# Low key rows of each quad copied by a small DMA of SyncE's queue, and another order of the words ahead of chunk 2

## The chip, the cores and the metric

The kernel runs on one core of a Trainium2 chip. The core has five engines, each with its own queue of instructions worked off in order: TensorE (PE; the loading of its weights is shown apart as PEld), VectorE (DVE), ScalarE (ACT), GpSimd (POOL) and SyncE (SP), which only issues DMAs here; GpSimd issues DMAs too. The metric is the device time of one execution in microseconds, as the median of several runs.

## What is computed

The reference is an attention with a forget gate, followed by an MLP. Cut to what matters:

```python
q, k, v: (8, 8, 576, 64); f: (8, 8, 576); w_in: (512, 2048); w_out: (2048, 512)
cum   = cumsum(log(clip(f, 1e-4, 1)), axis=-1)
s     = q @ k.T / sqrt(64) + cum[..., :, None] - cum[..., None, :]
s     = where(above the diagonal, -1e9, s)
attn  = softmax(s) @ v
x     = attn as (8 * 576, 8 * 64)
h     = x @ w_in
out   = gelu_tanh(h) @ w_out              # (4608, 512)
```

The kernel takes the decay out of the softmax: exp(cum[q] - cum[k]) is a factor of the query, which cancels in the division, and a factor of the key, `wT = exp(-cum)` (with a constant shift), which is multiplied into the values (`vw`) and into the column that gives the denominator (`w_bf`).

## The kernel before

**Tiles.** The 64 heads are worked in 16 quads of four heads (quads 2b and 2b+1 are batch b). The 4608 rows of the MLP are worked in nine chunks of 512. A quad's queries and keys are loaded (L208), transposed by VectorE (L214), and multiplied by TensorE into scores in PSUM (L277) in rounds of up to 512 columns per head; ScalarE takes their exp into `pt` (L285); the triangles on the diagonal are cut either by GpSimd (L291) or by a product on VectorE (L321); then TensorE multiplies `pt` with `w_bf` (denominators) and with `vw` (values) at L333 (quads 0 and 1, in halves) or L347 (all others). VectorE transposes and inverts the denominators (L366 to L370) and writes the attention's output into `xT` (L379). The score tiles share a PSUM pool of two slots: a whole round takes both, half a round one.

**Low key rows.** Quads from 2 on pack the first 64 keys and the last 64 keys into blocks of their own. The block "low" has its keys in partitions 64 to 127, so the first 64 rows of the weighted values are wanted a second time, in those partitions: `copy_low` (L236) copies `vw[i % 2][0:64, 0]` to `vw[i % 2][64:128, LOW]`, once per quad, 14 times in all (quads 2 to 15). It reads what `make_vw` (L231) has written, and the value products of that quad (L347) read it.

**MLP.** The first product is L395 (L419 for chunk 0, in halves and quarters; L468 and L520 where seven products of sums stand for eight), its gelu is ScalarE's. The second product is L667 for chunk 0 and L600 for the others. The latter two are generators: they are pulled a few matmuls at a time, as filler between the attention's steps. Results go to HBM by SyncE (L625, L673).

**Loads.** q, k, both weights and batch 0 and 1 of v are issued by GpSimd, the rest of v by SyncE.

**The order by hand.** The whole program is a list of words, run once from left to right; each engine's queue gets its instructions in that order. After the setup come SETUP and FRONT (all up to chunk 1), then for the chunks 2 to 7 SECOND, STEADY (three times), FLUSH and LAST. The first number of a word is a quad, a chunk or a part:

| word | what | engine that it queues on |
|---|---|---|
| TQ.i, TK.i | transpose the queries, the keys of quad i | VectorE |
| S.i.r, H.i.r.g | round r of the scores of quad i, whole or heads 2g and 2g+1, with its exp | TensorE, ScalarE |
| M, m | cut triangles: M.i.r.keys, m.i.r.keys | GpSimd, VectorE |
| D.i, V.i.x, v.i.x | denominators; value product x (even or odd columns), with a third number the half of quads 0 and 1 | TensorE, then VectorE |
| VW.i, vw.i | weighted values | GpSimd, VectorE |
| CL.i | `copy_low` | VectorE |
| CW | cumulative sums of log f (L719, L721) and their exp | TensorE, ScalarE |
| W | cast `wT` to `w_bf` | VectorE |
| TR, tr | cast the triangles for m | VectorE, ScalarE |
| Z | zeros in padding rows | GpSimd |
| J.h.g, j | quarter g of the first product of chunk 0 for its half h, with its gelu (j leaves the gelu to GJ) | TensorE, ScalarE |
| I.c.p | eighth p of the first product of chunk c, with its gelu | TensorE, ScalarE |
| F.c.n, f.c.n | n pulls of the second product of chunk c; F with weights of 128 columns, f with four of 32 | TensorE, then VectorE and SyncE |
| G, U, UW, PW, T | sums for the seven products, on VectorE (PW on GpSimd) | VectorE, GpSimd |
| LK.i, LQ.i, LP, LC, WI, WO | loads of keys, queries, v of batch 0, v of batch 1, w_in, w_out | GpSimd |
| LV, LB | loads of v | SyncE |
| B.n.cols | n filler matmuls of so many columns, whose result is not used (L256) | TensorE |
| X, Y | load ScalarE's table of exp, of gelu | ScalarE |

A word with @ waits for the end of another one. The code that runs a word:

```python
for word in table.split():
    word, _, gate = word.partition("@")
    name, *args = word.split(".")
    ...
    did = ops[name](*args)
    ...
    if gate:
        after(did[0], dmas[gate])
```

Of the kernel before, what the change touches and what calls it, by code (L numbers as in the profile page):

```python
# [16 lines left out]
def kernel(  # L17
# [10 lines left out]
    nc = tc.nc  # L28

    B, H, S, D = q.shape  # L30
# [36 lines left out]
    LOW, HIGH = NT, NT - 1  # L67
# [5 lines left out]
    """  # L73

    FRONT = """
        Z TQ.0 LP.2 TR WI.1 TQ.1 S.0.0 B.1.384 CW WI.0 TK.1 S.0.2 LP.4 LP.3 B.1.512 vw.0.0 B.2.512 H.1.0.1 H.1.1.1 WI.3 M.0.0 W vw.1.0 WI.2 B.2.512
        WI.5 LQ.2 WI.4 H.1.0.0 D.0.0 M.1.0.1 M.1.0.0 H.0.1.1 V.0.0.0 H.0.1.0 M.0.1 WI.6 V.0.1.0 B.2.256 H.1.1.0 B.1.256 D.1.0 H.0.3.0 B.1.256 V.1.0.0 H.0.3.1
        WI.7 LK.2 V.1.1.0 m.0.3.2 H.1.3.0 j.0.0 vw.0.1 H.1.3.1 LC.1.4 WO.0 m.0.3.4 WO.1 D.0.1 M.1.3 S.1.2 M.1.1 VW.1.1 V.0.0.1 V.0.1.1 LC.1.2 D.1.1
        J.0.1 J.0.2 WO.2 LC.1.0@VW.1.1 WO.3@m.0.3.2 V.1.0.1 V.1.1.1 LC.1.1 GJ.0.0 LC.1.3 TK.2 J.1.1 LK.3 J.0.3 J.1.0 LQ.3 TQ.2 LQ.4 VW.3
        J.1.3 LK.4 J.1.2 F.0.4 X F.0.4 S.2.0 F.0.11 TK.3 S.2.2 F.0.6 LV.2.0 TQ.3 F.0.4 LK.5 S.2.1 F.0.2 F.0.7 TQ.4 m.2.1 S.3.0 vw.2 CL.2 M.2.2 f.0.7  # L80
        M.2.0 D.2 S.3.1 f.0.7 LQ.5 V.2.0 m.3.0 S.3.2 TK.4 LK.6@LQ.4 f.0.1 f.0.3 V.2.1 M.3.2 f.0.2 S.4.1 CL.3 m.3.1 LQ.6 f.0.5 TQ.5 H.4.2.1 D.3 H.4.0.1
        H.4.0.0 VW.4 V.3.1 v.3.0 f.0.1 H.4.2.0 U.0 m.4.1 LV.2.1@m.3.1 I.1.1 LQ.7@CL.3 I.1.4 TQ.6 I.1.6 m.4.2.3 I.1.0 m.4.2.2 I.1.5 CL.4 U.3 LV.3.0@LQ.7
        U.1 TK.6 I.1.2 M.4.0 U.2 G.0 TK.5 UW.2.1 I.1.3 I.1.7 G.1.1.2 F.1.16 X UW.2.2 S.5.0 UW.2.3 LQ.8 F.1.19 S.5.1 D.4 VW.5 M.5.0 f.1.13 S.5.2 V.4.0
        f.1.14 V.4.1 UW.2.4 m.5.2.3 m.5.2.2 CL.5 M.5.1 S.6.0 f.1.13 D.5 S.6.1 f.1.4 LK.7 V.5.1 f.1.3 f.1.10 vw.6 S.6.2 m.6.1 M.6.2.2 m.6.0 V.5.0
        LV.3.1@LK.6 f.1.5 CL.6 LK.8 m.6.2.3
    """

    SECOND = """
# [32 lines left out]
    def many(n, shape, dtype, name):  # L121
        return [singles.tile(shape, dtype, name=f"{name}{i}") for i in range(n)]
# [11 lines left out]
    vw = many(2, [128, NT + 1, 4, D], BF16, "vw")  # L134
# [98 lines left out]
            wT[:, i, t0:t1, :].unsqueeze(3).to_broadcast([128, t1 - t0, 4, D]))  # L233

    def copy_low(i):
        return nc.vector.tensor_copy(vw[i % 2][64:128, LOW], vw[i % 2][0:64, 0])  # L236

    def key_columns(i, key, h, c):

# [511 lines left out]
    def load_values(b, half):  # L751
# [16 lines left out]
        "VW": lambda i, *part: make_vw(i, nc.gpsimd, *part),  # L768
        "vw": lambda i, *part: make_vw(i, nc.vector, *part),
        "CL": copy_low,  # L770
        "TK": transpose_k,
        "TQ": transpose_q,
# [86 lines left out]
```

## Time and profile before

| | |
|---|---|
| median of three runs | 323.59 us (323.31 to 323.96) |
| the profiled execution | 323.22 us |
| its span, first to last instruction | 321.4 us |
| granted TensorE clock | 1.000 |
| TensorE busy | 309.6 us |
| VectorE busy | 242.0 us |
| ScalarE busy | 212.7 us |
| GpSimd busy | 107.8 us |
| L236, the copy of the low key rows | 14 times, 0.22 us each |

Times are microseconds from the start of the span. A row of a timeline has the start, the time until the last of the merged instructions ended, the engine, the line, the operation, output and inputs, and the number of instructions; in brackets stands the idle time of the engine before it and what ended it. Matmuls overlap, so the time that a group costs TensorE is read from its start to the start of the next group. In lists of groups a row ends with the busy time in us and the mean of one in ns. In lists of DMA issues the last number is the median time from issue to landing, in us.

Where the words lie in time: quads 0 and 1 take TensorE from 8.6 to 31.9 us, the rest of the first product of chunk 0 until 40.7, quads 2 and 3 with the second product of chunk 0 until 66.2, the first product of chunk 1 until 80.1, quads 4 and 5 and part of 6 with the second product of chunk 1 until 100.7. With the first product of chunk 2 the list SECOND begins.

### The profile page before, as it was taken

What the parts mean: (1) busy time and instruction counts of PE and PEld (TensorE: products, weight loads), DVE (VectorE), ACT (ScalarE), POOL (GpSimd) and SP (SyncE); (2) the same over time, 40 slices, a digit from 0 to 9 for tenths busy, and PEclk for the clock granted to TensorE, in tenths of its full rate; (3) what the DMA queues carried; (4) which work ended last, traced back from release to release, by engine and by line L of the source; (5) the groups of instructions that cost most, each with busy time, mean ns of one, the idle gap of its engine ahead of it and who ended that gap; (6) DMA issues with size and microseconds to landing.
All of it is one profiled execution on the core that took longest, in us unless ns stands there. A gap on an engine that the chain in (4) does not pass through costs nothing.

```text
span 321.4 us, 11820 instructions
## 1 busy us (share of the span) xinstructions
PE 309.6 (96%) x5339; PEld 220.7 (69%) x5339; DVE 242.0 (75%) x374; ACT 212.7 (66%) x242; POOL 107.8 (34%) x145
## 2 busy tenths in 40 slices
PE   0899999999999999999999999999999999999996
PEld 0557844544776567776788878767776786688785
DVE  4765337898979879779877987699876866597674
ACT  4676576775766776878767866787586744836610
POOL 8989343522301416400851075205610140000000
PEclk9999999999999999999999999999999999999999
DMA  7999999585126931593139411971011111010203
GB/s 126 218 210 208 247 213 199 104 155 109 35 43 129 227 78 37 116 209 72 39 82 228 87 39 35 190 172 36 7 47 53 37 34 37 30 37 0 100 33 99
DMA packets 47490, 33.41 MB, mean 104 GB/s; under 512 B 29776, under 2 KB 42192, under 8 KB 47440
## 3 DMA queue, kind: packets, MB, share of 16 engines
q0 software_dynamic: 9632, 15.99, 28.3%
q1 hardware_dynamic: 37664, 16.60, 19.1%
q8 instruction: 41, 0.67, 0.9%
q14 instruction: 9, 0.07, 0.1%
q10 hardware_dynamic: 144, 0.07, 0.1%
HBM read 36.85 MB, written 9.44 MB: 144 GB/s over the span
## 4 chain that ended last, share of the span: by engine, by line
PE 91%; ACT 3%; DVE 3%; DMA 2%; issue 1%; POOL 0%; DVEq 0%; POOLq 0%
PE ps_w L600 30%; PE ps_h L395 19%; PE ps_s L277 9%; PE po L347 9%; PE ps_q L520 8%; PE pso L667 4%; PE ps_h L419 4%; PE ps_u L468 4%; DMA q_c<-in_q_dram 2%; PE po_m L333 1%; ACT pt L285 1%; ACT gT L403 1%; DVE xT L379 1%; PE idle_ps L256 1%; PE cum_ps L721 1%
## 5 line engine op out<-in xcount | busy, mean ns | idle before, releaser
L285 ACT ACTIVATE pt<-ps_s 128x1024 bf16<-128x1024 f32 (+2 forms) x100 | 94.0, 990 | 38.6 <-PE ps_s L277 35.9
L291 POOL TENSOR_SCALAR_AFFINE_SELECT pt<-pt 128x512 bf16<-128x512 bf16 (+3 forms) x65 | 41.4, 647 | 95.2 <-ACT pt L285 72.3
L395 PE MATMUL ps_h<-xT,w_in_sb 128*128 128x512 bf16 (+1 forms) x320 | 66.8, 358 | 0.3 <-ACT gT L403 0.2
L395 PEld LDWEIGHTS <-w_in_sb 128*128 128x128 bf16 x320 | 31.2, 98 | 26.6 <-issue 0.6
L600 PEld LDWEIGHTS <-gT 128*32 128x32 bf16 (+1 forms) x1216 | 44.1, 97 | 5.5 <-issue 2.2
L403 ACT ACTIVATE gT<-ps_h 128x1024 bf16<-128x1024 f32 x34 | 34.6, 1017 | 18.7 <-PE ps_h L395 18.4
L600 PE MATMUL ps_w<-w_out_sb,gT 128*32 128x256 bf16 (+1 forms) x1008 | 42.6, 273 | 0.0
L277 PE MATMUL ps_s<-qT,kT 32*128 32x64 bf16 (+5 forms) x896 | 36.3, 263 | 3.2 <-DVE qT L214 3.0
L600 PEld LDWEIGHTS <-gsum 128*32 128x32 bf16 (+1 forms) x948 | 35.4, 97 | 3.8 <-issue 1.5
L231 POOL TENSOR_TENSOR vw<-v_nat,wT 128x1280 bf16<-128x1280 f32 (+1 forms) x13 | 29.6, 2279 | 11.7 <-DMA v_nat<-in_v_dram 11.4
L536 DVE TENSOR_TENSOR usnap<-ps_q,usnap 128x1024 f32<-128x1024 f32 x15 | 17.9, 1222 | 18.6 <-PE ps_q L520 13.2
L277 PEld LDWEIGHTS <-kT 32*128 32x128 bf16 x896 | 16.5, 93 | 19.6 <-issue 10.1
L600 PE MATMUL ps_w<-usum,gsum 128*32 128x256 bf16 (+1 forms) x791 | 30.0, 273 | 0.0
L617 DVE COPY snap<-ps_w 128x512 f32<-128x512 f32 x32 | 21.8, 681 | 6.2 <-PE ps_w L600 6.0
L531 ACT ACTIVATE gT<-usnap 128x1024 bf16<-128x1024 f32 x15 | 15.8, 1054 | 12.1 <-DVE usnap L536 11.8
L379 DVE TENSOR_TENSOR xT<-po,rb 128x576 bf16<-128x576 f32 x26 | 19.5, 752 | 5.6 <-PE po L347 5.3
L347 PE MATMUL po<-pt,vw 128*32 128x64 bf16 (+4 forms) x624 | 22.4, 278 | 0.0
L214 DVE STREAM_TRANSPOSE qT<-q_c 128x576 f32<-128x576 f32 x16 | 19.8, 1246 | 1.7 <-DMA q_c<-in_q_dram 1.7
L347 PEld LDWEIGHTS <-vw 128*32 128x32 bf16 x672 | 14.6, 97 | 9.4 <-issue 2.8
L214 DVE STREAM_TRANSPOSE kT<-k_c 128x576 f32<-128x576 f32 x16 | 19.5, 1246 | 1.9 <-DMA k_c<-in_k_dram 1.9
L208 POOL DMA_DIRECT2D k_c<-in_k_dram x16 | 9.1, 568 | 33.6 <-DVE kT L214 18.0
L520 PEld LDWEIGHTS <-w_in_sb 128*128 128x128 bf16 x160 | 15.6, 98 | 2.5 <-issue 0.4
(135 smaller groups left out, 478.5 us busy)
## 6 DMA issues: line engine op xcount, KB each, us to landing
out_dram<-o_st SPq DMA_DIRECT2D x35, 256.0 KB, 2.3
k_c<-in_k_dram POOLq DMA_DIRECT2D x16, 288.0 KB, 5.3
q_c<-in_q_dram POOLq DMA_DIRECT2D x16, 288.0 KB, 6.3
v_nat<-in_v_dram SPq DMA_DIRECT2D x16, 256.0 KB, 5.4
v_nat<-in_v_dram SPq DMA_DIRECT2D x20, 128.0 KB, 5.1
v_nat<-in_v_dram POOLq DMA_DIRECT2D x8, 256.0 KB, 8.1
w_in_sb<-in_moe_w_in_dram POOLq DMA_DIRECT2D x8, 256.0 KB, 7.8
w_out_sb<-in_moe_w_out_dram POOLq DMA_DIRECT2D x4, 512.0 KB, 11.3
```

Source lines behind the costliest of these rows:

```text
L214: return nc.vector.transpose(out=dst.rearrange("p s c -> p (s c)").bitcast(FP32) .rearrange("p (t a) -> p a t", a=S // 32), in_=src.rearra ...
L231: return eng.tensor_mul(vw[i % 2][:, t0:t1], vb[:, t0:t1, h0:h0 + 4, :], wT[:, i, t0:t1, :].unsqueeze(3).to_broadcast([128, t1 - t0, 4, D]))
L277: nc.tensor.matmul(tiles[h // 2][:, h % 2, c0:c0 + nq], key_columns(i, key, h, c), qq[32 * h:32 * h + 32, q0:q0 + nq, c], start=(c == 0 an ...
L285: nc.scalar.activation(p[:, 2 * g:2 * g + 2, off:off + n], t[:, :, 0:n], AF.Exp, scale=scale)
L291: nc.gpsimd.affine_select(out=x, in_=x, compare_op=ALU.is_ge, fill=0.0, base=0, pattern=pattern, channel_multiplier=-1)
L347: nc.tensor.matmul(po[r0:r0 + w.shape[-1], 448 + q0:448 + q0 + nq], w, p[:, h, col:col + nq], start=(key in (0, "low")), stop=(key in ("lo ...
L379: nc.vector.tensor_mul(xT[:, 2 * u + x, r0 + s0:r0 + s1], po, rbs[i, part])
L395: nc.tensor.matmul(ph[:, j, n * cols:(n + 1) * cols], w_in_sb[:, dt, 128 * ft:128 * ft + 128], xT[:, dt, h0:h0 + cols], start=(dt == 0 and ...
L403: nc.scalar.activation(gelus(c, 2 * pr, 2), ph, AF.Gelu_apprx_tanh)
L520: nc.tensor.matmul(ps[:, k, HC * n:HC * n + HC], w[:, d, 128 * n:128 * n + 128], x[:, d, :], start=(first and n == 0 and d == 0), stop=(d ...
L600: nc.tensor.matmul(ps[c0:c0 + width, n, cols[0]:cols[1]], x[:, j, 128 * n + c0:128 * n + c0 + width], w[:, j, cols[0]:cols[1]], start=(fir ...
L617: copy(kept[name], ps)
```

## The change

`copy_low` issues a DMA in SyncE's queue, where it was a copy on VectorE. This holds for all 14 quads. The list FRONT is replaced by another one; SETUP, SECOND, STEADY, FLUSH and LAST stay. The new FRONT has the same loads, scores, products and sums, with these differences in kind: the triangles are cast by ScalarE (tr for TR); M.0.0, M.0.1, M.2.2 and M.5.0 become m; m.2.1, m.3.1, m.4.2.2, m.4.2.3, m.5.2.3, m.6.0, m.6.1 and m.6.2.3 become M; UW.2.1 becomes PW.2.1; there are 21 filler words B with 6,912 columns in all for 7 with 3,968; pulls of the second products are split into smaller pieces.

```diff
     FRONT = """
-        Z TQ.0 LP.2 TR WI.1 TQ.1 S.0.0 B.1.384 CW WI.0 TK.1 S.0.2 LP.4 LP.3 B.1.512 vw.0.0 B.2.512 H.1.0.1 H.1.1.1 WI.3 M.0.0 W vw.1.0 WI.2 B.2.512
-        WI.5 LQ.2 WI.4 H.1.0.0 D.0.0 M.1.0.1 M.1.0.0 H.0.1.1 V.0.0.0 H.0.1.0 M.0.1 WI.6 V.0.1.0 B.2.256 H.1.1.0 B.1.256 D.1.0 H.0.3.0 B.1.256 V.1.0.0 H.0.3.1
-        WI.7 LK.2 V.1.1.0 m.0.3.2 H.1.3.0 j.0.0 vw.0.1 H.1.3.1 LC.1.4 WO.0 m.0.3.4 WO.1 D.0.1 M.1.3 S.1.2 M.1.1 VW.1.1 V.0.0.1 V.0.1.1 LC.1.2 D.1.1
-        J.0.1 J.0.2 WO.2 LC.1.0@VW.1.1 WO.3@m.0.3.2 V.1.0.1 V.1.1.1 LC.1.1 GJ.0.0 LC.1.3 TK.2 J.1.1 LK.3 J.0.3 J.1.0 LQ.3 TQ.2 LQ.4 VW.3
-        J.1.3 LK.4 J.1.2 F.0.4 X F.0.4 S.2.0 F.0.11 TK.3 S.2.2 F.0.6 LV.2.0 TQ.3 F.0.4 LK.5 S.2.1 F.0.2 F.0.7 TQ.4 m.2.1 S.3.0 vw.2 CL.2 M.2.2 f.0.7
-        M.2.0 D.2 S.3.1 f.0.7 LQ.5 V.2.0 m.3.0 S.3.2 TK.4 LK.6@LQ.4 f.0.1 f.0.3 V.2.1 M.3.2 f.0.2 S.4.1 CL.3 m.3.1 LQ.6 f.0.5 TQ.5 H.4.2.1 D.3 H.4.0.1
-        H.4.0.0 VW.4 V.3.1 v.3.0 f.0.1 H.4.2.0 U.0 m.4.1 LV.2.1@m.3.1 I.1.1 LQ.7@CL.3 I.1.4 TQ.6 I.1.6 m.4.2.3 I.1.0 m.4.2.2 I.1.5 CL.4 U.3 LV.3.0@LQ.7
-        U.1 TK.6 I.1.2 M.4.0 U.2 G.0 TK.5 UW.2.1 I.1.3 I.1.7 G.1.1.2 F.1.16 X UW.2.2 S.5.0 UW.2.3 LQ.8 F.1.19 S.5.1 D.4 VW.5 M.5.0 f.1.13 S.5.2 V.4.0
-        f.1.14 V.4.1 UW.2.4 m.5.2.3 m.5.2.2 CL.5 M.5.1 S.6.0 f.1.13 D.5 S.6.1 f.1.4 LK.7 V.5.1 f.1.3 f.1.10 vw.6 S.6.2 m.6.1 M.6.2.2 m.6.0 V.5.0
-        LV.3.1@LK.6 f.1.5 CL.6 LK.8 m.6.2.3
+        LC.1.4 B.1.256 WI.4 B.1.256 TQ.0 B.1.256 TK.1 B.1.128 tr CW B.1.512 B.1.256 S.0.2 B.1.512 B.1.128 TQ.1 LP.2 LP.3 H.1.0.1 WI.1 S.0.0 B.1.256 B.1.256 B.1.256 B.1.128 B.1.512 B.1.256 B.1.128 H.1.1.1 B.2.512 vw.0.0 vw.1.0 m.0.0 B.2.512 WI.0 W H.1.0.0 H.0.1.0 D.0.0 B.1.128 B.1.128 V.0.0.0 LQ.2 LP.4 H.0.1.1 WI.5 B.1.256 V.0.1.0 Z WI.2 M.1.0.0 H.1.1.0 M.1.0.1 B.1.256 D.1.0 H.0.3.0 V.1.0.0 H.0.3.1 m.0.1 V.1.1.0 WI.6 WI.7 WO.0 H.1.3.0 WI.3 M.1.1 j.0.0 H.1.3.1 m.0.3.2 LK.2 m.0.3.4 vw.0.1 D.0.1 WO.3 V.0.0.1 M.1.3 WO.1 S.1.2 V.0.1.1 VW.1.1 J.0.2 D.1.1 WO.2 GJ.0.0 J.0.3 V.1.0.1 V.1.1.1 J.0.1 J.1.3 J.1.0 TQ.2 TK.2 U.0 J.1.2 LC.1.1 LK.3 LC.1.0@VW.1.1 F.0.3 LC.1.2 F.0.1 X LC.1.3 F.0.1 S.2.0 f.0.1 LQ.3 LK.4 f.0.1 F.0.1 TK.3 F.0.5 LQ.4 F.0.3 S.2.2 F.0.4 U.1 F.0.1 TQ.3 F.0.1 J.1.1 VW.3 LQ.5 vw.2 LK.5 F.0.4 m.2.2 f.0.1 S.2.1 f.0.1 TQ.4 f.0.1 CL.2 f.0.1 M.2.1 f.0.2 TK.4 f.0.1 F.0.1 M.2.0 LQ.6 F.0.1 f.0.4 S.3.0 CL.3 f.0.5 D.2 f.0.2 S.3.1 f.0.5 V.2.0 f.0.1 S.3.2 LK.6 M.3.1 f.0.5 TQ.5 V.2.1 f.0.1 S.4.1 F.0.1 M.3.2 F.0.1 m.3.0 F.0.2 TK.5 F.0.1 H.4.2.1 D.3 H.4.0.1 H.4.0.0 V.3.1 LV.2.0 v.3.0 f.0.1 LQ.7@CL.3 H.4.2.0 TK.6 U.2 I.1.4 I.1.0 I.1.5 I.1.3 U.3 LV.2.1 PW.2.1 I.1.1 M.4.0 VW.4 M.4.2.3 I.1.2 I.1.7 m.4.1 I.1.6 F.1.6 CL.4 TQ.6 G.0 F.1.7 S.5.0 G.1.1.2 F.1.4 UW.2.2 F.1.3 UW.2.3 F.1.5 LV.3.0@LQ.7 m.5.0 F.1.9 M.4.2.2 F.1.1 S.5.1 f.1.3 VW.5 f.1.4 D.4 f.1.6 S.5.2 f.1.2 V.4.0 f.1.3 M.5.2.3 f.1.1 UW.2.4 f.1.3 LK.8 M.5.1 f.1.6 V.4.1 S.6.0 m.5.2.2 f.1.1 LV.3.1 f.1.3 LQ.8 f.1.2 LK.7 D.5 f.1.2 M.6.0 f.1.5 CL.5 f.1.1 S.6.1 f.1.10 V.5.1 M.6.1 f.1.2 vw.6 f.1.1 X f.1.4 S.6.2 M.6.2.3 M.6.2.2 CL.6 f.1.1 V.5.0 f.1.1 F.1.1
     """
...
     def copy_low(i):
-        return nc.vector.tensor_copy(vw[i % 2][64:128, LOW], vw[i % 2][0:64, 0])
+        return nc.sync.dma_start(out=vw[i % 2][64:128, LOW], in_=vw[i % 2][0:64, 0])
```

## The prediction

> **What bounds the kernel.** I read the shares of the engines first, then the busy time by stretches, then TensorE's, VectorE's and ScalarE's timelines of the first 66 us, and last the loads' landings. Two lines of the page and four stretches (us; then busy us and instructions of PE, PEld, DVE, ACT, POOL; granted clock; DMA share; GB/s):
>
> ```profile
> PE 309.6 (96%) x5339; PEld 220.7 (69%) x5339; DVE 242.0 (75%) x374; ACT 212.7 (66%) x242; POOL 107.8 (34%) x145
> PE 91%; ACT 3%; DVE 3%; DMA 2%; issue 1%; POOL 0%; DVEq 0%; POOLq 0%
> ...
> 14.50:24.00 9.50, 9.48 (x150) 5.15 (x153) 6.43 (x16) 7.89 (x10) 8.71 (x14) 1.00 1.19 216
> 24.00:40.60 16.60, 16.43 (x240) 13.53 (x233) 6.67 (x12) 10.35 (x11) 9.79 (x13) 1.00 1.20 229
> 40.60:66.20 25.60, 25.56 (x457) 12.18 (x455) 17.46 (x25) 18.81 (x21) 12.15 (x16) 1.00 0.81 163
> 132.00:230.00 98.00, 98.00 (x2058) 74.45 (x2060) 81.06 (x115) 73.61 (x80) 38.41 (x47) 1.00 0.49 107
> ```
>
> From 14.5 us on TensorE has next to no idle time: 0.02 us of 9.5, 0.17 of 16.6, 0.04 of 25.6, none of 98. The stretches between read the same. So an edit shortens the kernel only if it takes work or a wait out of TensorE's own queue, and whatever it adds there is paid in full. VectorE (75%) has slack. What is not packed is the head:
>
> ```profile
> 8.62 0.83 PE L277 MATMUL ps_s<-qT,kT 32*128 32x256 bf16 x16 [2.96 <-DVE qT L214]
> 9.67 1.27 PE L719 MATMUL cum_ps<-logfT,utri_f 128*128 128x320 f32 x2
> 10.74 1.85 PE L721 MATMUL cum_ps<-logfT,ones_f 128*128 128x64 f32 x8
> 12.52 0.46 PE L277 MATMUL ps_s<-qT,kT 32*128 32x320 bf16 x8
> ...
> 5.96 0.20 ACT L703 COPY logfT<-ps_lt 64x64 f32<-64x64 f32 x1
> ...
> 10.92 1.26 DVE L214 STREAM_TRANSPOSE qT<-q_c 128x576 f32<-128x576 f32 x1 [1.59 <-DMA q_c<-in_q_dram]
> ```
>
> TensorE sits idle until quad 0's queries are transposed (8.62), then spends 2.85 us (9.67 to 12.52) on the cumulative sums, whose input was ready at 6.16. Quad 1's queries land at 10.92 and are usable at 12.18.
>
> **The copy of the low key rows.** Removed: 14 VectorE copies. Added: 14 issues in SyncE's queue, each behind the value product it reads (L231) and ahead of whatever SyncE has next.
>
> ```profile
> L236 DVE COPY vw<-vw 64x256 bf16<-64x256 bf16 x14 | 3.1, 224 | 0.4
> out_dram<-v_nat SPq DMA_DIRECT2D x1, 64.0 KB, 1.7
> out_dram<-o_st SPq DMA_DIRECT2D x35, 256.0 KB, 2.3
> v_nat<-in_v_dram SPq DMA_DIRECT2D x20, 128.0 KB, 5.1
> ...
> 153.45 2.34 POOL L231 TENSOR_TENSOR vw<-v_nat,wT 128x1280 bf16<-128x1280 f32 x1
> ```
>
> VectorE gets 14 x 0.22 = 3.1 us back, worth 0 while TensorE is packed. The price hangs on the landing. No copy inside SBUF is in the trace; the nearest rows are the small store (1.7 us) and, from the other side, the v loads (5.1). At 32 KB it is nearest to the small store, so I take about 2. In a steady chunk GpSimd finishes the product at 155.8, SyncE's earlier store went out at 155.1, so the copy goes out at 155.9 and lands at 157.9; its first reader is the matmul group at 160.44. Cover: 2.5 us; at 5.1 it would be gone and each of the five odd quads from 7 to 15 would pay up to 0.6. Even quads' copies are read only in the next chunk. Behind the waiting issue stand result stores; the next one there goes out at 165.2, long after the wait ends at 161.3. Sum of this part: 0 (0 to +4).
>
> **The head, walked through.** Words now run: fillers, CW, S.0.2, H.1.0.1, S.0.0, H.1.1.1, and so on. Durations are start to next start in TensorE's rows: S.0.2 0.39, S.0.0 0.76, a half round H 0.34 to 0.56, a D or V half 0.28, j 1.85, a 256-column filler between other work 0.21 (19.84 to 20.05); an exp starts some 0.55 after a half round and holds ScalarE 0.7 to 1.0.
> - CW starts at 6.2 and ends at 9.05; three quarters of 2.85 us are now in idle time. S.0.2 follows (9.5 to 9.9).
> - H.1.0.1 needs quad 1, ahead of whose queries the same three loads stand as before: 12.23. Its exp runs from 12.78 to 13.59.
> - S.0.0, first in line before, now stands behind it and needs two slots of the score PSUM, one of them H.1.0.1's: it can finish at 13.6 + 0.76 = 14.36. Its exps end at 15.26 and 15.97.
> - H.1.1.1 waits for the first of them: 15.28 to 15.84. Four 512-column fillers follow (2 took 0.54 before; four some 0.97): 16.81. Then H.1.0.0 0.34, H.0.1.0 0.56: 17.71.
> - The rest is TensorE's own work: 3 x 0.21 of filler, two D and four V halves 6 x 0.28, three half rounds H.0.1.1, H.1.1.0, H.0.3.0 (0.56, 0.56, 0.45), H.0.3.1 0.44, H.1.3.0 0.45, j 1.85, H.1.3.1 0.45: 7.07, so 24.78.
> In the trace H.1.3.1 ends at 23.80. So the head loses about 0.95: the saved sums are eaten by quad 1's load, the slot wait and longer fillers. From below: with no slot wait at all TensorE's work from 12.23 is 11.35, end 23.58, a gain of 0.2. I take +0.9, since waits of this kind show in the trace. The triangles now cast by ScalarE (three copies, 0.2 to 0.37 each) end near 7, ahead of CW's exp: 0.
>
> **Up to chunk 1.** The same matmuls follow, in another order. What changes is how often TensorE changes the shape of its array (128*128, 128*32, 32*128):
>
> ```profile
> 54.57 1.69 PE L667 MATMUL pso<-w_out_sb,gT 128*32 128x512 bf16 x28
> 56.09 0.85 PE L347 MATMUL po<-pt,vw 128*32 128x512 bf16 x24
> ...
> 60.10 1.26 PE L667 MATMUL pso<-w_out_sb,gT 128*32 128x512 bf16 x20
> 61.30 0.63 PE L277 MATMUL ps_s<-qT,kT 32*128 32x320 bf16 x8
> ```
>
> 28 matmuls with the same shape next take 1.52, 0.054 each; 20 with another shape next take 1.20, where 20 x 0.054 is 1.09: a change costs 0.11. Counted in the words, runs of one shape from S.2.0 to the first I go from 19 to 23 (f and F now alternate): 4 x 0.11 = +0.44. Between D.0.1 and S.2.0 there are two more, +0.22, against the 0.15 stall before D.1.1 (26.38 to 26.53), which J.0.2 now fills: +0.07, say +0.05.
>
> J.1.1 moves behind the exps of S.2.2, so ScalarE loads its tables twice more, 1.28 each (the row at 41.90), and does the gelu between: 3.6 us. Over it lie 17 pulls of the chunk 0 filler (0.22 each, 3.7 us) and S.2.1, until S.3.0 needs both slots: cover just enough, +0.1 (0 to 1). The Trainium skill (ScalarE: Activation LUTs, What ACT_TABLE_LOAD costs) puts a switch at 2.66 us, the load with a drain of 1.38. Here an ACTIVATE follows the 1.28 load at once (148.92, then 150.21), so the trace bears out the load alone; by the Trainium skill S.2.1's exps would be 2.8 later and the sum an estimated 1.7 higher.
>
> The loads stay one saturated queue (DMA share 1.19 and 1.20 above). At the trace's spacing (w_in 1.35 us a piece, w_out 2.5) WI.3 lands near 31, J.0.1 starts near 33; w_out's third piece near 40, wanted near 42. Hidden, 0. Chunk 1 has as many runs of one shape as before, and VectorE less to do (masks and one weight sum go to GpSimd, 34% busy): 0. From chunk 2 on no word changes.
>
> **Sum:** +0.9 +0.05 +0.44 +0.1 = +1.5. The profiled execution took 323.22 (span 321.4 and 1.8 around it), which gives 324.7; the median of the three is 323.59, 0.37 above it: 325.1. I predict 325.0, its own range 324.2 to 325.9.
>
> **Rivals.** 0.2% of the time, 0.65 us, is about what a measurement can tell from no change.
> - *No change* (about 323.6): shape changes hide under ScalarE's pace and the slot waits are shorter than walked; head -0.2 to +0.2, the rest +0.2. For: ScalarE is 83% busy from 14.5 to 24 us. Against: 25.56 of 25.60 us are TensorE's own. 20%.
> - *Faster*: the sums leave the chain for good. If quad 1's queries were usable by 9.9, TensorE's 11.35 would end at 21.2, a gain of 2.6; with the +0.6 behind it, 321.6. It decides from 2.2 us earlier than the trace's 12.18. For: 2.96 us of idle time stand in the row at 8.62. Against: the loads ahead of quad 1 are unchanged. 16%.
> - *Late copies*: landings behind other traffic take 5 us or more, five odd quads' V waits 0.6 each and the loaded head adds 1: 325.0 + 4 = 329. Against: stores of 256 KB land in 2.3. 6%.
> - *Slow first matmuls*: CW at half speed takes 5.7, ends at 11.9; S.0.2 and its exps end near 14, H.1.0.1 starts 1.6 later: 326.6. The Trainium skill (TensorE: Matmul & The Clock Gate, Part 1) says just this of the first 3.4 us after idling. The trace disagrees: granted clock 1.00, and S.0.0 at 8.62, straight after idling, took 0.76, no more than two half rounds later (0.44 each). 8%.
> The forecast has 50%, some 4 of them within the bound. Faster 0.16 and a little from the second tail: 0.17; within 0.2% 0.23; slower 0.60. Range 322.8 to 326.8: below it most of the faster case, above it the late copies.
>
> **What will show it.** The end of H.1.3.1 near 24.8 (23.8 now) and an exp gap of 0.8 ahead of S.0.0 bear out the head; its end by 23.4 would sink the forecast. The first I of chunk 1 should start near 67.7 (66.25 now), with TensorE as packed as before. The idle time before L347 should name no DMA of vw; if it does, the late copies are true. A CW longer than 2.9 shows slow matmuls.

## The result and the profile after

The changed kernel takes 327.97 us in the median (326.50 to 330.24), the kernel before 323.59 beside it: 1.0133 times as long, with a 95% interval of 1.0106 to 1.0160. It is slower by 4.4 us. The forecast was 325.0 with a range up to 326.8: the side is right, the size is not. Here and below, a ratio leaves out executions more than 1.5% above the fastest of the same kernel, while medians and ranges count all.

The profiled execution is the median run itself, 327.97, with a span of 326.0 (321.4 before). All line numbers lie nine lower (L277 is L268, L347 is L338, L256 is L247, L719 and L721 are L710 and L712, L419 is L410). From the page, shares and chain:

```profile
PE 314.5 (96%) x5370; PEld 222.8 (68%) x5370; DVE 238.0 (73%) x354; ACT 216.0 (66%) x247; POOL 112.4 (34%) x148
PE 91%; ACT 3%; DMA 2%; DVE 2%; issue 1%; POOL 1%; POOLq 0%; DVEq 0%
```

At this height little has changed: VectorE is busy for 4.0 us less, TensorE, ScalarE and GpSimd for 3 to 5 us more. The stretches tell more (same columns as before: busy us and instructions of PE, PEld, DVE, ACT, POOL; granted clock; DMA share; GB/s):

```profile
14.50:24.00 9.50, 9.50 (x129) 4.45 (x128) 5.68 (x16) 7.50 (x10) 7.69 (x15) 0.83 1.15 201
...
43.20:69.00 25.80, 25.77 (x462) 13.04 (x455) 19.84 (x25) 20.33 (x22) 11.47 (x15) 1.00 0.81 163
...
83.00:101.45 18.45, 18.45 (x518) 13.57 (x516) 15.21 (x25) 12.60 (x14) 4.59 (x8) 1.00 0.52 100
101.45:102.62 1.17, 0.00 (x2) 0.00 (x1) 0.23 (x1) 1.17 (x2) 0.00 (x0) 1.00 0.63 173
...
136.00:234.00 98.00, 97.99 (x2044) 74.29 (x2046) 79.59 (x110) 73.45 (x80) 38.34 (x47) 1.00 0.50 109
```

Two things are new: a granted clock of 0.83 in the head, where it was 1.00, and 1.17 us near 102 in which TensorE does nothing. Before, that part had no idle time:

```profile
80.00:100.70 20.70, 20.70 (x557) 15.58 (x555) 18.73 (x32) 14.91 (x16) 3.59 (x6) 1.00 0.22 50
```

The rest is packed as it was. Set against the starts of the same work in both traces, the loss falls in three places (the last column is the experiment e9 below):

| start of | before | after | lost since the row above | predicted | e9 |
|---|---|---|---|---|---|
| the first j (J of chunk 0) | 21.50 | 23.75 | +2.25 | +0.95 | +0.34 |
| the first I of chunk 1 | 66.25 | 69.07 | +0.57 | +0.59 | +0.57 |
| the first I of chunk 2 | 100.69 | 105.03 | +1.52 | 0 | 0.00 |
| the last matmul | 318.30 | 322.67 | +0.03 | 0 | +0.04 |

TensorE's timeline of the head (start, time until the last ended, operation, count, idle time ahead and what ended it):

```profile
6.25 1.38 PE L710 MATMUL cum_ps<-logfT,utri_f 128*128 128x320 f32 x2
7.43 2.55 PE L712 MATMUL cum_ps<-logfT,ones_f 128*128 128x64 f32 x8
...
12.24 0.57 PE L268 MATMUL ps_s<-qT,kT 32*128 32x256 bf16 x10 [0.73 <-DVE qT L205]
13.66 0.52 PE L268 MATMUL ps_s<-qT,kT 32*128 32x256 bf16 x14 [0.85 <-ACT pt L276]
14.11 1.56 PE L247 MATMUL idle_ps<-idle 128*128 128x256 bf16 x7
15.61 1.03 PE L268 MATMUL ps_s<-qT,kT 32*128 32x320 bf16 x8
16.57 1.56 PE L247 MATMUL idle_ps<-idle 128*128 128x512 bf16 x4
18.07 0.97 PE L268 MATMUL ps_s<-qT,kT 32*128 32x256 bf16 x16
...
23.75 1.92 PE L410 MATMUL ps_h<-xT,w_in_sb 128*128 128x256 bf16 x16
```

The same work in the trace of before:

```profile
15.08 0.61 PE L256 MATMUL idle_ps<-idle 128*128 128x512 bf16 x2
15.62 0.51 PE L277 MATMUL ps_s<-qT,kT 32*128 32x256 bf16 x8
...
16.34 0.63 PE L277 MATMUL ps_s<-qT,kT 32*128 32x320 bf16 x8
16.90 0.35 PE L333 MATMUL po_m<-pt,vw 128*32 128x256 bf16 x8
```

Four 512-column fillers take 1.50 from start to start (16.57 to 18.07), where two took 0.54 before (15.08 to 15.62); a half round takes 0.96 (15.61 to 16.57), where it took 0.56 (16.34 to 16.90). From 18.07 on the matmuls have their old length: two half rounds take 0.89. Two stretches cut where the record of the clock changes:

```profile
10.80:14.20 3.40, 1.82 (x35) 0.88 (x28) 1.71 (x2) 2.13 (x4) 1.56 (x3) 1.00 1.15 210
14.20:17.70 3.50, 3.50 (x18) 1.55 (x19) 2.27 (x6) 2.51 (x3) 3.40 (x8) 0.51 1.14 215
```

For one stretch of 3.41 us (14.27 to 17.68 by the trace's record of the clock) TensorE had half its clock, straight after 3.4 us in which it was busy for 1.82 only: the waits for quad 1's queries (0.73) and for a slot that H.1.0.1's exp had to free (0.85) lie there, 1.58 together.

The other loss, inside V.5.0:

```profile
100.85 0.60 PE L338 MATMUL po<-pt,vw 128*32 128x512 bf16 x10
102.62 0.51 PE L338 MATMUL po<-pt,vw 128*32 128x448 bf16 x10 [1.17 <-issue]
```

"Issue" says that no engine and no transfer of data had to end; the group is cut in its middle. What was missing is TensorE's own code. The traces have a DMA queue of the kind "instruction", q8, with 42 packets of 16 KB in the changed kernel; TensorE has 10,749 rows of matmuls and weight loads there, 256 for each packet. In the changed kernel TensorE stops after 10 of the 24 matmuls of V.5.0. In e5 below, which has 8 more fillers ahead of it, it stops after 2; in e3, which has 13 fewer, after 23. All three, and e2, stop behind the same number of weight loads, 1,503, and e7 behind 1,247, two packets' worth earlier (256 weight loads with as many matmuls). So it is not a place in the program at which TensorE stops but the end of a packet of code.

The DMA queues in the 4 us from 95 to 99, after and then before (packets, MB, share of 16 engines):

```profile
q0 software_dynamic: 236, 0.49, 87.2%
q1 hardware_dynamic: 5, 0.00, 0.5%
```
```profile
q8 instruction: 1, 0.02, 1.6%
```

Before, the code was alone on the queues. After, quad 8's keys, quad 8's queries and quad 7's keys (issued from 93.7 to 96.0) fill them, and no packet of code starts. Starts of the packets of q8, read from the traces:

```
kernel   packets of q8 start at (us)          last one landed   TensorE idle
before    88.4   92.2   96.0  100.2                             none
after     90.8   94.7   99.9                  101.24            101.45 to 102.62
e2        90.9   94.4  102.7                  103.61            101.59 to 105.22
e5        88.4   92.2   99.0                   99.88             99.35 to 101.41
e7        83.5   91.4                          92.41             92.25 to  93.86
e9        88.3   91.7   95.6   99.9                             none
```

On time they follow each other here by 3.4 to 4.3 us. Where the next came only after 5.2 to 8.3 us, TensorE ran dry and went on 1.4 to 1.6 us after it had landed. The pause alone doesn't decide it: ahead of 90.8 the changed kernel has one of 9.1 us without idle time, in which TensorE gets through 346 rows of matmuls and weight loads; ahead of the late packets there were 372 (after) to 469 (e2). Nor does all traffic count alike: from 89 to 92 us, with the values' load on q1 at a share of 0.6 to 0.9, the packet at 90.8 came without idle time behind it. In the late cases loads of keys and queries (q0) fill the queues, in e7 values too. The Trainium skill (Runtime: NRT & Kernel Launch, Instruction fetch mechanics) says that code comes in blocks of 256 instructions by a queue of the engine's own, and that the cost of crossing into the next block is mostly hidden. The blocks agree with these traces; "mostly hidden" fails in the four kernels of the table with idle time, and in e3.

### The profile page after: what moved, and what is told of

The parts are those of the page before. It is cut to its first block, busy times and chain, and to the rows that moved or that the text cites. A ratio compares the mean times of both kernels' runs of the same rounds, so it can differ in the third digit from the quotient of the medians.

```text
span 326.0 us, 11900 instructions
## 1 busy us (share of the span) xinstructions
PE 314.5 (96%) x5370; PEld 222.8 (68%) x5370; DVE 238.0 (73%) x354; ACT 216.0 (66%) x247; POOL 112.4 (34%) x148
## 4 chain that ended last, share of the span: by engine, by line
PE 91%; ACT 3%; DMA 2%; DVE 2%; issue 1%; POOL 1%; POOLq 0%; DVEq 0%
PE ps_w L591 29%; PE ps_h L386 19%; PE ps_s L268 9%; PE po L338 9%; PE ps_q L511 8%; PE pso L658 5%; PE ps_h L410 4%; PE ps_u L459 4%; DMA q_c<-in_q_dram 2%; PE po_m L324 1%; PE idle_ps L247 1%; ACT pt L276 1%; ACT gT L394 1%; PE ps_p L591 0%; DVE xT L370 0%
## 5 line engine op out<-in xcount | busy, mean ns | idle before, releaser
L282 POOL TENSOR_SCALAR_AFFINE_SELECT pt<-pt 128x512 bf16<-128x512 bf16 (+3 forms) x67 | 43.9, 664 | 107.6 <-ACT pt L276 83.3
L268 PE MATMUL ps_s<-qT,kT 32*128 32x64 bf16 (+5 forms) x896 | 36.4, 263 | 1.6 <-ACT pt L276 0.8
L222 POOL TENSOR_TENSOR vw<-v_nat,wT 128x1280 bf16<-128x1280 f32 (+1 forms) x13 | 30.6, 2350 | 5.0 <-PE ps_s L268 4.6
L268 PEld LDWEIGHTS <-kT 32*128 32x128 bf16 x896 | 16.8, 93 | 18.1 <-issue 10.5
L338 PE MATMUL po<-pt,vw 128*32 128x64 bf16 (+4 forms) x624 | 22.7, 278 | 1.2 <-issue 1.2
L338 PEld LDWEIGHTS <-vw 128*32 128x32 bf16 x672 | 14.9, 97 | 10.3 <-issue 3.8
```

The costliest lines, as they stand in the source:

```text
L222: return eng.tensor_mul(vw[i % 2][:, t0:t1], vb[:, t0:t1, h0:h0 + 4, :], wT[:, i, t0:t1, :].unsqueeze(3).to_broadcast([128, t1 - t0, 4, D]))
L268: nc.tensor.matmul(tiles[h // 2][:, h % 2, c0:c0 + nq], key_columns(i, key, h, c), qq[32 * h:32 * h + 32, q0:q0 + nq, c], start=(c == 0 an ...
L282: nc.gpsimd.affine_select(out=x, in_=x, compare_op=ALU.is_ge, fill=0.0, base=0, pattern=pattern, channel_multiplier=-1)
L338: nc.tensor.matmul(po[r0:r0 + w.shape[-1], 448 + q0:448 + q0 + nq], w, p[:, h, col:col + nq], start=(key in (0, "low")), stop=(key in ("lo ...
```

## The experiments

All were timed beside the kernel before, which had medians of 323.7 to 323.9 each time.

**e1, e2: the two halves of the change.**

```diff
 e1: FRONT as before
     def copy_low(i):
-        return nc.vector.tensor_copy(vw[i % 2][64:128, LOW], vw[i % 2][0:64, 0])
+        return nc.sync.dma_start(out=vw[i % 2][64:128, LOW], in_=vw[i % 2][0:64, 0])
 e2: FRONT as changed, copy_low as before
```

> The kernel before with the low rows copied by SyncE's DMA and the old words. Theory 'words' (the order alone made the kernel slower): 323.3 to 324.0 us, granted clock 1.000, no idle time of TensorE ahead of a value product. Rival 'copy' (the DMA itself costs time, by late landings or by the traffic it adds): 324.8 us or more, with idle time ahead of the value products.

> The changed kernel with the copy back on VectorE. Theory 'words': as the changed kernel, 326.5 to 328.5 us, some runs at clock 0.993 to 0.995 and some at 1.000. Rival 'copy': 325.5 us or less, and no 1.2 us of idle time inside V.5.0.

Measured: e1 325.75 (325.16 to 327.32), ratio 1.0062 (1.0039 to 1.0085); e2 330.20 (327.43 to 336.66), ratio 1.0161 (1.0121 to 1.0200). TensorE's waits in e1 (us in total, times, longest):

```profile
PE po L347 <- DMA vw<-vw: 1.0, 1, 1.0
```

With the old words the copy has a price: quad 2's product ended at 53.9, its copy went out then, and V.2.0 stood for it from 57.0 to 58.0. That is 1.0 of the 1.9 us; another 0.55 stands already at the first j, ahead of any copy (see the end of this document). In the changed kernel no instruction of TensorE waits for a copy. e2 shows that the copy isn't what costs there: the new words alone are at least as slow. They are slower than the expected 326.5 to 328.5; in e2's profile the idle time in V.5.0 is longer and has a second price:

```profile
105.22 0.50 PE L349 MATMUL po<-pt,vw 128*32 128x448 bf16 x10 [3.63 <-issue]
...
106.40:109.70 3.30, 3.30 (x15) 2.02 (x14) 1.43 (x3) 0.00 (x0) 0.00 (x0) 0.50 0.23 79
```

After 3.63 us without work the clock is halved for another 3.4 us.

**e3, e4: the words cut behind H.1.3.1.** Both with the DMA copy.

```diff
 e3: FRONT = old words up to H.1.3.1, then the new words
 e4: FRONT = new words up to H.1.3.1, then the old words
```

> The old words up to H.1.3.1, then the new ones, copy by DMA. Theory 'head' (the new words up to H.1.3.1 cost 0.8 us at full clock and 1.5 more where the clock is halved after quad 1's wait; the rest costs 0.9 and a 1.2 us stall in V.5.0): 324.5 without the stall to 325.7 us with it, clock 1.000 in every run, end of H.1.3.1 at 23.8. Rival 'rest' (the later words carry the loss): 326.5 us or more.

> The new words up to H.1.3.1, then the old ones, copy by DMA. Theory 'head': 324.4 us in runs at clock 1.000, 325.9 us in runs at 0.993 to 0.995, and both kinds occur. Rival 'rest': 323.3 to 324.2 us in all runs.

Measured: e3 326.79 (324.99 to 329.17), ratio 1.0097 (1.0065 to 1.0129); e4 331.25 (327.81 to 333.88), ratio 1.0194 (1.0152 to 1.0237). By its median e3 falls to the rival 'rest': the later words carry most of the loss. Its profile is of its fastest run (324.99); what the slower ones lost beyond it was not traced. This profile has the old head (+0.12 at the first j), the same +0.58 up to chunk 1, and again idle time in V.5.0 (0.5): the second loss is made by the rest of the words, not handed down from the head. e4 lies outside both expectations and answers less, since the cut made waits of its own:

```profile
PE ps_h L420 <- DMA w_in_sb<-in_moe_w_in_dram: 3.4, 1, 3.4
PE po L348 <- DMA vw<-vw: 2.0, 1, 2.0
```

The new head loads w_in's piece 3 last, the old rest needs it first. As a measure of the head it is void.

**e5: more fillers in the two waits of the head** (four matmuls of 512 columns each).

```diff
-... TQ.1 LP.2 LP.3 H.1.0.1 WI.1 S.0.0 ...
+... TQ.1 B.4.512 LP.2 LP.3 H.1.0.1 B.4.512 WI.1 S.0.0 ...
```

> The changed kernel with two more fillers (one 128x512 matmul each) in TensorE's two waits of the head: one behind S.0.2, where it waits for quad 1's queries, and one behind H.1.0.1, where it waits for a slot of the probabilities. Theory clock: the profile of the changed kernel was halved to a granted clock of 0.5 from 14.26 to 17.68 us because TensorE was busy for only some 0.5 to 0.85 of the 3.4 us before it. With the fillers no such stretch appears, the granted clock is 1.000 in nearly all runs, the first instruction of J starts at 22.3 to 22.6 us in place of 23.75, and the times are 326.3 to 327 in place of 326.5 to 330.2. The idle stretch of TensorE in V.5.0 stays as it is. Rival: the halved stretch doesn't come from idle TensorE, so it stays in the same runs, and the two fillers add their own 0.2 us each: a median of 327.9 or more.

In the run each wait has four matmuls, not the one that the expectation names. Its 0.5 to 0.85 us of busy time ahead of the halving is a misreading: the row of 10.80 to 14.20 in the section above has 1.82.

Measured: 327.46 (326.81 to 329.61), ratio 1.0116 (1.0090 to 1.0143), between the two ranges. The head did what the clock theory says: no halved stretch, and the first j at 21.87. The sum did not, because V.5.0 took the gain back in the same run:

```profile
14.00:18.00 4.00, 3.92 (x53) 2.03 (x54) 2.41 (x7) 3.59 (x5) 3.56 (x9) 1.00 1.14 219
...
101.41 1.30 PE L349 MATMUL po<-pt,vw 128*32 128x512 bf16 x18 [2.06 <-issue]
```

A head that ends earlier meets the same loads; the idle time grew from 1.17 to 2.06, and the clock was at half from 101.19 to 104.60. The runs at a clock of 1.000 took 326.8 to 327.6.

**e6, e7: the loads ahead of V.5.0, moved both ways.** e6 is the changed kernel, e7 the kernel before.

```diff
 e6:
-... UW.2.3 F.1.5 ... LK.8 M.5.1 ... LV.3.1 f.1.3 LQ.8 f.1.2 LK.7 D.5 ... f.1.10 V.5.1 ... V.5.0 f.1.1 ...
+... UW.2.3 LQ.8 F.1.5 ... M.5.1 ... f.1.3 f.1.2 D.5 ... f.1.10 LK.7 V.5.1 ... V.5.0 LV.3.1@LK.6 LK.8 f.1.1 ...
 e7:
-... UW.2.3 LQ.8 ... V.4.1 ... S.6.0 f.1.13 D.5 S.6.1 f.1.4 LK.7 V.5.1 ... V.5.0 LV.3.1@LK.6 f.1.5 CL.6 LK.8 ...
+... UW.2.3 ... LK.8 V.4.1 ... S.6.0 LV.3.1 f.1.13 LQ.8 LK.7 D.5 S.6.1 f.1.4 V.5.1 ... V.5.0 f.1.5 CL.6 ...
```

Among the new words four loads have also lost their gates. With its word e6 gives LV.3.1 its gate back (@LK.6), and e7 takes it away.

> The changed kernel with four words that issue loads (LQ.8, LK.7, LV.3.1, LK.8) put back to where the old order has them, behind and around V.5.0 and UW.2.3; all else as in the changed kernel. Theory traffic: TensorE stands still inside V.5.0 because the next part of its instructions arrives late, behind the big loads that the new words start at 89 to 96 us. With these loads later no idle stretch without a wait is left in V.5.0, and the kernel is 1 to 3.6 us faster than the changed one: 325 to 326.8. Rival density: the instructions arrive late since the new order has more short matmuls in that stretch; the idle stretch stays at 1 us or more and the time at 327 to 329.

> The kernel before (VectorE's copy, its own order of TensorE's work) with the same four loads put to where the new order has them: LK.8 ahead of V.4.1, LV.3.1 behind S.6.0, LQ.8 and LK.7 ahead of D.5. Theory traffic: an idle stretch of TensorE of 0.5 to 4 us that names no engine and no transfer appears at 97 to 104 us, and the kernel takes 324.5 to 327.5. Rival density: the loads are hidden as before, no such stretch, 323.2 to 324.2.

Measured: e6 326.60, ratio 1.0082 (1.0064 to 1.0099); e7 326.41 (325.44 to 327.95), ratio 1.0078 (1.0055 to 1.0101). Three runs of e6 took 326.52, 326.54 and 326.60 at a clock of 0.995, which fits one halved window left in the head. Two others took 331.67 and 333.63 at 0.974 and 0.968; in the latter, the profiled one, the half clock of the head lasted 20.5 us. No idle time is left in V.5.0 of e6, nor in e9 below with the same loads. In e7 one appears where the kernel before has none:

```profile
93.86 0.40 PE L600 MATMUL ps_w<-w_out_sb,gT 128*32 128x256 bf16 x8 [1.61 <-issue]
```

It ended 3 us ahead of the stretch expected, two packets of code earlier. Taking the loads away takes the idle time away, and adding them to the old order, with its old density of matmuls, makes it: the loads are the cause, and the density theory is out. Which of the four it takes was not tested.

**e8: only the sums first.** The kernel before, with the sums ahead of S.0.0.

```diff
-Z TQ.0 LP.2 TR WI.1 TQ.1 S.0.0 B.1.384 CW WI.0 TK.1 S.0.2 LP.4 LP.3 B.1.512 vw.0.0 B.2.512 H.1.0.1 ...
+Z TQ.0 LP.2 tr WI.1 TK.1 TQ.1 B.3.256 CW S.0.0 WI.0 S.0.2 LP.4 LP.3 B.2.512 vw.0.0 H.1.0.1 ...
```

> The kernel before (VectorE's copy) with only this of the new head: CW (the running sums of the gates) ahead of S.0.0, quad 1's keys transposed ahead of its queries, the fillers around them split. Theory: S.0.0 is then the first thing that waits for quad 0's transposes, CW's 2.85 us lie in a wait that was filled by fillers, and the head ends up to 0.8 us earlier: 322.6 to 323.4. Rival: CW runs at half clock there (3.5 us) and pushes S.0.0 back, the head ends 0.3 to 1.5 us later: 323.9 to 325.1.

Measured: 329.51 (328.75 to 330.08), ratio 1.0171 (1.0153 to 1.0190): outside both. The first j starts 4.8 us later. One stretch of e8, then the same of the kernel before:

```profile
14.00:18.00 4.00, 3.67 (x36) 1.66 (x38) 1.77 (x5) 2.59 (x4) 2.63 (x4) 1.00 1.16 215
```
```profile
14.00:18.00 4.00, 3.93 (x66) 1.92 (x65) 2.96 (x8) 3.96 (x6) 3.99 (x7) 1.00 1.16 227
```

With nearly as much busy time TensorE gets through 36 matmuls in place of 66, at a clock that the column gives as 1.00. The record of the clock in e8 has its first entry at 28.52 us (11.74 before, 10.85 after), and ahead of a first entry the column reads 1.00 whatever the clock is. The matmuls say that it was about half: two 512-column fillers take 0.97 in e8 (13.04 to 14.01), 0.54 before.

**e9: both repairs at once**, e5's fillers and e6's loads in the changed kernel.

> The changed kernel with both repairs at once: the two fillers in the head's waits, and the four words of loads where the old order has them. Theory: the two losses are separate and add up, the halved clock of the head some 1.8 us and the late instructions of V.5.0 1.2 to 3.6 us, so neither shows in the profile, the granted clock is 1.000, and what is left against the kernel before is the head's slot wait (+0.4 at the first instruction of J) and the array's changes of shape (+0.6 up to chunk 1): 324.6 to 325.2. Rival: a third cost is left in the new order, or the one repair brings the other loss back elsewhere: 325.8 or more.

Measured: 325.32 (324.57 to 325.77), ratio 1.0046 (1.0027 to 1.0066), 0.1 above what was expected. All seven runs lie at a clock of 0.998 to 1.000. The head's stretch:

```profile
14.50:24.00 9.50, 9.48 (x144) 5.32 (x144) 7.30 (x19) 7.81 (x10) 9.10 (x16) 1.00 1.19 211
```

The table above has its starts: +0.34 in the head, +0.57 up to chunk 1, nothing behind. So the two faults make up some 2.65 of the loss (327.97 less 325.32), and 1.4 is left (325.32 less the 323.90 of the kernel before beside it), of which the trace shows 0.94. The 0.57 up to chunk 1 comes back alike in the changed kernel, e2, e3 and e5. The 0.34 of the head is no shown loss: four traces with the old head (e1, e3, e7, e11) have their first j at 21.63 to 22.05, the one before at 21.50, and e9 at 21.84. Each repair alone brought less (0.5 with e5, 1.4 with e6), because the idle time in V.5.0 changes with the head ahead of it.

**e10, e12: a warm start for the kernel before.** Its own order and copy, with six fillers in the 2.96 us ahead of S.0.0; e12 has TK.1 earlier as well.

```diff
-... WI.1 TQ.1 S.0.0 B.1.384 CW WI.0 TK.1 S.0.2 ...
+... WI.1 TQ.1 B.6.512 S.0.0 B.1.384 CW WI.0 TK.1 S.0.2 ...        (e10)
+... WI.1 TK.1 TQ.1 B.6.512 S.0.0 B.1.384 CW WI.0 S.0.2 ...        (e12)
```

> The kernel before with six fillers (128x512 matmuls on the idle tile) ahead of S.0.0, in the 2.96 us that TensorE waits for quad 0's transposes; nothing else is changed. Theory: in the kernel before the first matmuls run at half speed (S.0.0 0.76, CW 2.85) since TensorE has stood idle, and fillers there make it fast sooner: S.0.0 and CW take 0.4 to 1.4 us less together, and the head ends 0.4 to 1.3 us earlier: 322.4 to 323.4. Rival: the first matmuls ran at full speed, as the prediction took it, or the head is paced by quad 1's queries and the exps: 323.6 to 324.4.

> The kernel with six fillers ahead of S.0.0, and TK.1 (quad 1's keys transposed, by VectorE) ahead of TQ.1: quad 1's keys land at 9.3 us and its queries at 10.9, so VectorE can do the keys while it waits for the queries. Theory: the 0.97 us that H.1.0.1 waited for the keys is gone, H.1.0.1 starts at 12.2 to 12.7 in place of 13.36, limited by the slots of the probabilities, and the head ends 0.6 to 1.0 us earlier than with the fillers alone: 322.2 to 322.9, faster than the kernel before. Rival: the wait only changes its name (a slot, the values' load), or the clock falls in the wait: 323.2 or more.

Measured: e10 323.36 (322.75 to 327.34), ratio 0.9998 (0.9970 to 1.0026); e12 323.43 (322.38 to 326.78), ratio 1.0004 (0.9975 to 1.0033). TensorE's rows in e10:

```profile
8.71 0.52 PE L277 MATMUL ps_s<-qT,kT 32*128 32x256 bf16 x16 [0.27 <-DVE qT L214]
...
9.33 0.70 PE L719 MATMUL cum_ps<-logfT,utri_f 128*128 128x320 f32 x2
9.87 1.37 PE L721 MATMUL cum_ps<-logfT,ones_f 128*128 128x64 f32 x8
...
13.36 0.97 PE L277 MATMUL ps_s<-qT,kT 32*128 32x256 bf16 x16 [0.97 <-DVE kT L214]
```

S.0.0 takes 0.45 from start to start (8.71 to 9.16, where a filler starts) in place of 0.76, and CW 1.84 (9.33 to 11.17) in place of 2.85. That is 1.3 us saved, of which the first j keeps 0.57: the head then waits for quad 1's keys. With the keys first (e12) that wait is gone, but the j comes no earlier, since ScalarE has become the pace: its seven exps from S.0.2 on follow without a gap,

```profile
12.36 5.76 ACT L285 ACTIVATE pt<-ps_s 128x640 bf16<-128x640 f32 x7
```

5.75 us before as well. Ten of e10's twelve runs lie between 322.75 and 324.40; two took 327 at a clock of 0.984. A gain of 0.5 us is thus seen in the median and not shown over all runs. e12 falls to its rival: the wait only changed its name. No kernel tried beats the kernel before by more than the measurement can tell.

**e11: the copy with an earlier product.**

```diff
-... LV.2.0 TQ.3 F.0.4 LK.5 S.2.1 F.0.2 F.0.7 TQ.4 m.2.1 S.3.0 vw.2 CL.2 M.2.2 ...
+... LV.2.0 TQ.3 vw.2 CL.2 F.0.4 LK.5 S.2.1 F.0.2 F.0.7 TQ.4 m.2.1 S.3.0 M.2.2 ...
```

> The kernel before with the DMA copy in place of VectorE's, and with vw.2 and CL.2 (quad 2's value product and its copy) some 3 us earlier in the words, behind TQ.3. Theory: the copy by DMA costs nothing by itself, and the whole price of the copy alone (1.0 us of wait in V.2.0) came from quad 2's late product: no wait on the copy is left, 323.5 to 324.5. Rival: landings behind other transfers cost elsewhere too, 325 to 326 as with the copy alone.

Measured: 324.59 (323.89 to 326.35), ratio 1.0027 (1.0011 to 1.0043). Most of e1's price is gone, though a wait is left, on TensorE's weight loads:

```profile
57.01 0.47 PEld L347 LDWEIGHTS <-vw 128*32 128x32 bf16 x20 [0.55 <-DMA vw<-vw]
```

This copy went out at 51.09 and landed near 57.0: 5.9 us for 32 KB, behind the loads of values, keys and queries. It cost TensorE 0.24 (V.2.0 from 0.79 to 1.03), and 0.27 more as an echo: VectorE takes up V.2.0's result that much later, then transposes quad 4's keys, and S.4.1 waits for them. So the copy alone isn't free in the old order: up to chunk 1, 0.5 stays of the 1.1 that e1's trace loses there behind the head, and the late product was the larger part.

## Why the prediction was half right

Two steps of the sum failed. The head, +0.9, was walked with full-speed durations, though two waits stand in the new one; behind them the clock was at half for 3.41 us, and the head lost 2.25. And chunk 1 stood in the sum with 0, though the new words draw four loads together in it; TensorE's code came late behind them, 1.52.

**TensorE is packed, so only its own queue counts: right.** Both losses are waits or slower matmuls of TensorE, and the 4 us that VectorE got back are worth nothing.

**The copy, 0 (0 to +4): right for the changed kernel, for a narrower reason.** Its copies land in 1.7 to 4.7 us (median 2.7), where about 2 was taken, and none is waited for. The cover was worked out in a steady chunk, though, and the thin place is quad 2: e1 pays 1.0 there. The bound of 5.1 was passed too, by the 5.9 in e11.

**The head, +0.9: the waits right, the clock missing.** The walk holds up to 14.11: H.1.0.1 starts at 12.24 (12.23 foreseen), S.0.0 ends at 14.11 (14.36). From 18.96 to the end of H.1.3.1, at 26.05, are 7.09 (7.07). Nearly the whole miss lies between (18.96 where 17.71 was foreseen), where fillers and half rounds ran at half clock. With that gone (e9) the first j is 0.34 late, not 0.95; 0.45 of the difference is luck, since quad 1's queries came that much earlier in that run (H.1.0.1 at 11.79).

**The rival of slow first matmuls, 326.6 at 8%, was thrown out with a false argument.** It was right that the start is slow, though wrong in where it hurts. CW took 3.52 (6.25 to 9.77), by the test set up for it more than 2.9; this cost nothing, as S.0.2 was done before quad 1's queries were there. What costs is that the clock, once up, was taken back after the two waits. The argument against was that S.0.0, straight after idling, took no longer than two half rounds, at a clock of 1.00. But at full clock a whole round takes no longer than a half round, though it has twice the matmuls: e10's S.0.0 took 0.45, a half round 0.44. So the 0.76 was slow. And the 1.00 stood ahead of the first record. The Trainium skill (TensorE: Matmul & The Clock Gate, Part 1) has a slow start and free-running windows of 3.4 us. The traces agree: every entry of the record lies a multiple of 3.413 us behind the one before. It speaks of an idle window; here one with TensorE busy for 1.82 of 3.40 us was followed by half the clock.

**Up to chunk 1, +0.05 +0.44 +0.1: right in sum.** Measured +0.57, and again +0.57 in e9 and +0.58 in e3. The three terms weren't tested apart, so how well the sum fits may be luck. The rival of no change, which had shape changes hidden, is out by it.

**The other rivals.** Late copies: not in the changed kernel; with the old words one wait of 1.0, at quad 2 and not at the odd quads that the rival named (e1). Faster: it needed quad 1's queries by 9.9; they were usable at 12.24, as before.

**The loads, "hidden, 0", right for the weights; chunk 1, "0": wrong, +1.52.** In the changed kernel no instruction of TensorE waits for w_in or w_out. Chunk 1 got its 0 from the runs of one shape and from VectorE's and GpSimd's work; the four loads that the new words draw together there (LK.8, LV.3.1, LQ.8 and LK.7) stand in no term and no rival. No wait of TensorE names their data. What the prediction left out is what else uses the queues meanwhile: TensorE's code does, and these loads stood where a packet of it was due.

**Open:** why the half clock of the head lasted 3.4 us in some runs and 20.5 in one of e6's; what decides whether it comes at all (two of the changed kernel's five runs have a clock of 1.000); and whether the code is late for the bytes ahead of it, for the number of transfers or for the queue that they use. No run tells these apart.

## What to carry to other kernels

When loads are moved into a stretch that had few, look at the packets of the instruction queue there: idle time put down to "issue" in the middle of a group can be code that came late. Here it stood at the end of a packet each time, and it went when the loads did. A wait that is cheap by itself can cost the next 3.4 us half their clock, so fillers belong into each wait of a cold head, the new ones too. Read a clock of 1.00 against the duration of a matmul whose full speed is known, above all near the start.

## What the hardware showed beyond that

- A granted clock of 1.00 at the start can mean "not recorded": e8's matmuls ran at half speed until 28.5 us under it.
- Idle time from late code can cost twice: 3.63 us in e2 were followed by 3.4 us at a clock of 0.50, 2.06 us in e5 likewise; 1.17 us in the changed kernel and 1.61 in e7 were not.
- The record of the clock divides a trace into windows of 3.41 us. Of the windows at full clock, in all traces, half the clock followed each in which TensorE was busy for 1.73 us or less (in e2 1.58 and 1.12, in e5 1.58, in e6 1.73), and none with 1.98 or more. Near 1.8 both happen: the 1.84 of the changed kernel (10.85 to 14.27) were followed by it, 1.81 in e4 and 1.80 in e7 were not. So busy time alone doesn't decide, and the changed kernel lies at the border.
- One head, five traces: the later the record of the clock begins, the later the first j. It begins at 11.74 (before), 11.85 (e3), 12.36 (e11), 12.83 (e7) and 13.81 us (e1), and the first j starts at 21.50, 21.63, 21.99, 22.02 and 22.05. Half a microsecond in the head is thus no more than the spread between runs.
- A copy of 32 KB inside SBUF by SyncE's queue landed in 1.7 to 4.7 us in the changed kernel and in 5.9 us once in e11, with loads of values, keys and queries under way; VectorE took 0.22.
